# Loading v in longer runs, and transposing the exponentials through DRAM

## The chip, the cores and the metric

The kernel runs on one core of a Trainium2 chip. The metric is device time in microseconds (us), as a median of runs.

## The reference

Two attention steps and a feed-forward layer, in float32. For each of 8 batches and 8 heads, with 576 positions of 64 numbers, 32 learned rows p attend to k and v and give a packed result of 32 rows. Then each of the 576 rows of q attends to that packed result, which is both its keys and its values. The heads are laid side by side (512 numbers a position), and a layer follows with three input matrices of 512 x 768, of which the elementwise maximum is taken, and one output matrix.

```
p_packed = sm_attn(p, k, v)
out = sm_attn(q, p_packed, p_packed)
x = out.transpose(0, 2, 1, 3).reshape(B * S, H * D)
h = np.maximum(np.maximum(x @ w1, x @ w2), x @ w3)
return h @ w_out
```

## The kernel before

The work is cut by batch (8 of them). For each batch a chain of stages runs, each with a letter: S scores of p against k (line 253), A their softmax weights without the division (exponentials at line 271), then the exponentials are transposed, V their product with v (line 337), K the packed result turned, Q scores of q against it (line 366), B the second softmax (lines 389 to 412), P the packed result times the input weights (line 439), N the product of the second softmax with that (line 475, the largest part of TensorE's work), E the elementwise maximum, which moves N's sums out of PSUM into `r` (lines 486 and 489), H the operands of the output layer, O and F that layer and its stores (lines 544, 563, 573). N and O are done in two float32r parts each, a high and a low one.

The order of all instructions is written out by hand as two strings of words, START for batches 0 and 1 and the beginning of batch 2, and LOOP for each further pass. A word lets one stage take one step. A digit is the batch relative to the pass (X1 in LOOP is the spread of the next batch), and a letter v, g or a behind it chooses VectorE, GpSimd or ScalarE. Each engine works off its instructions in that order. Loads and stores stand in the same order and are all issued by SyncE.

The exponentials of batches 0 and 1 are transposed by TensorE (`turn`). Those of batches 2 to 7 go through `spread`, word X, in three steps. The first two let VectorE transpose all 32 x 32 blocks of one half of the heads (line 313) into the tile `x`. The third issues sixteen transfers (line 319) that move the blocks of `x`, partition group by partition group, into the tile `xt`, where they stand as V needs them. A block row there is 2 x 32 numbers, so each run of such a transfer is 256 B long. V multiplies slices of `xt` with v.

v of one batch and half of the heads is loaded by two transfers: `va`, 512 positions as 128 partitions of 4 KB, read as four runs of 1 KB a partition (line 165), and `vb`, the last 64 positions (line 166). The weights come as blocks of 512 KB, w00 to w52 for the input matrices and w60 to w65 for the output matrix (line 153), and are turned to float32 by four instructions each, on ScalarE (lines 188 and 193), VectorE (line 202) and GpSimd (line 206). q of one batch comes as two loads of 576 KB (line 174), called q20 and q21 for batch 2.

Tiles live in rotating buffers. k, v, q, `x`, `xt` and `r` share eight of them, and the staged weights share six with the output layer's operands. A load waits on SyncE until the earlier holder of its buffer has been read for the last time, and everything behind it on SyncE waits too. In START, around the third step of X2, SyncE's order is v21, v20, w42, w52, w51, the sixteen transfers, w64, w62, w65, q20, w63, w60, q21, w61.

Of the kernel before, what the change touches and what calls it, by code (L numbers as in the profile page):

```python
# [10 lines left out]
F32 = mybir.dt.float32  # L11
# [9 lines left out]
B, H, S, D, NP = 8, 8, 576, 64, 32  # L21
DM, DF = 512, 768
P = 128
G = 2
R = 2
# [3 lines left out]
SF = 4  # L29
# [3 lines left out]
NT = S // NP  # L33
# [3 lines left out]
NX, NB, NY = 6, 8, 21  # L37
# [51 lines left out]
def fused_kernel(ctx: ExitStack, tc: tile.TileContext, kp, qt, va, vb, wi, wo, out):  # L89
# [14 lines left out]
    nc = tc.nc  # L104

    const = ctx.enter_context(tc.tile_pool(name="const", bufs=1))
    pool = ctx.enter_context(tc.tile_pool(name="pool", bufs=1))
    ps_big = ctx.enter_context(tc.tile_pool(name="ps_big", bufs=2, space=PSUM))
    ps_moe = ctx.enter_context(tc.tile_pool(name="ps_moe", bufs=4, space=PSUM))

    ident = const.tile([P, P], F32, name="ident")
    make_identity(nc, ident)

# [48 lines left out]
    def load_v(b, g):  # L162
        u = b * G + g
        v = pool.tile([P, SF + 1, 256], F32, name=f"v{u}", tag="b", bufs=NB)
        nc.sync.dma_start(out=v[:, 0:SF, :], in_=va[u].rearrange("p (t x) -> p t x", x=256))
        nc.sync.dma_start(out=v[0:SR, SF, :], in_=vb[u])
        loaded["v", b, g] = v

# [72 lines left out]
    s1, a1, z1, a1t, av, pp, s2, a2 = {}, {}, {}, {}, {}, {}, {}, {}  # L241
# [63 lines left out]
    def spread(b):  # L305

        x = pool.tile([P, NT, R, NP], F32, name=f"x{b}", tag="b", bufs=NB)
        for r in range(R):
            nc.vector.transpose(out=x[:, :, r], in_=a1[b, r][0].rearrange("p (t y) -> p t y", y=NP))
            yield 1
        at = pool.tile([P, SF + 1, 4, R, NP], F32, name=f"xt{b}", tag="b", bufs=NB)
        for c in range(4):
            n = len(range(c, NT, 4))
            for i in range(4):
                nc.sync.dma_start(out=at[NP * c:NP * c + NP, 0:n, i], in_=x[NP * i:NP * i + NP, c::4])
        for r in range(R):  # L320
            a1t[b, r] = at[:, :, :, r]
        yield 0

    def values(b, rs):
# [280 lines left out]
    def weigh_and_turn(b, r):  # L605
# [4 lines left out]

    stages = {
        "S": scores, "A": weigh_and_turn, "Z": invert, "X": spread, "V": lambda b, *rs: values(b, rs), "K": packed, "Q": queries,
        "B": attend, "C": convert, "P": project, "N": layer_in, "E": maximum, "H": halves,
        "O": layer_out, "F": finish, "W": weights,
    }
    loads = {"k": load_k, "v": load_v, "q": load_q, "w": load_w}
    begun = {}

# [69 lines left out]
```

## Time and profile before

| | |
|---|---|
| median of 3 runs | 475.94 us (475.03 to 477.21) |
| span of the profiled execution | 471.1 us |
| TensorE matmul, weight load | 453.5 us (96%), 404.0 us (86%) |
| VectorE, ScalarE, GpSimd | 346.9 us (74%), 171.7 us (36%), 207.0 us (44%) |
| DMA | 55.66 MB, 36580 packets, of which 17328 under 512 B |

The profiled execution is one of its own. Its span, from its first to its last instruction, is what the profile's times refer to; its time beyond the span is not recorded, and the median lies 4.8 us above the span. In the rows, PE is TensorE's matmul, PEld its weight load, DVE VectorE, ACT ScalarE, POOL GpSimd, and SPq the queue of SyncE, which issues the DMAs. "a<-b" behind an instruction names the tile that it writes and those that it reads.

### The profile page before, as it was taken

The page shows a single profiled execution, that of the slowest core. Times are in us where ns is not written, and L with a number is a line of the kernel's source. Part 1 is how long each engine was busy: PE and PEld are TensorE (multiplying, and loading weights), DVE is VectorE, ACT ScalarE, POOL GpSimd, SP SyncE. Part 2 cuts the span into 40 slices and gives each one's busy share as a digit, 9 for nine tenths or more (in the row PEclk, how much of TensorE's full clock was granted, in tenths as well). Part 3 has the DMA queues.
Part 4 walks back from the last instruction along what each step waited for, and adds up shares of the span by engine and source line. Part 5 has one row for each costly group of instructions (what it writes and reads, how often), then busy time and mean ns, then how long its engine had stood idle before and what let it go on. Part 6 is the DMA issues. An engine that isn't in the chain of part 4 may idle for free.

```text
span 471.1 us, 11501 instructions
## 1 busy us (share of the span) xinstructions
PE 453.5 (96%) x4714; PEld 404.0 (86%) x4714; DVE 346.9 (74%) x727; ACT 171.7 (36%) x333; POOL 207.0 (44%) x180
## 2 busy tenths in 40 slices
PE   8669997999999999999999999999999999999996
PEld 4346985989899898989989898998989898998996
DVE  1698897899996668786777678776787668875652
ACT  3277866653441226122350225212260223402330
POOL 0346863767243055612563037421556036531542
PEclk9989999999999999999999999999999999999999
DMA  8998947003025540083303730064300820020002
GB/s 297 401 379 274 309 124 282 2 1 113 26 78 163 175 128 1 25 281 58 104 1 102 229 114 24 27 199 126 118 1 34 283 36 3 26 76 1 1 5 97
DMA packets 36580, 55.66 MB, mean 118 GB/s; under 512 B 17328, under 2 KB 27568, under 8 KB 36528
## 3 DMA queue, kind: packets, MB, share of 16 engines
q1 hardware_dynamic: 36528, 54.93, 35.8%
q8 instruction: 37, 0.61, 0.5%
q14 instruction: 15, 0.12, 0.1%
HBM read 41.94 MB, written 9.44 MB: 109 GB/s over the span
## 4 chain that ended last, share of the span: by engine, by line
PE 93%; DVE 3%; DMA 2%; ACT 1%; issue 0%; POOL 0%; POOLq 0%; DVEq 0%
PE mi L475 48%; PE mo L544 29%; PE pw L439 7%; PE s L253 2%; DMA q<-in_qt 2%; PE av L337 2%; PE s L366 2%; PE s L143 1%; PE tp L296 1%; DVE e L389 1%; PE tp L143 1%; DVE xt L218 0%; PE pa L143 0%; PE pa L337 0%; DVE w_sb L202 0%
## 5 line engine op out<-in xcount | busy, mean ns | idle before, releaser
L475 PE MATMUL mi<-a2h,ph 128*128 128x288 f32 x576 | 174.3, 303 | 2.6 <-DVE r L489 2.1
L475 PE MATMUL mi<-a2h,pl 128*128 128x288 f32 x576 | 170.1, 295 | 0.0
L475 PE MATMUL mi<-a2l,ph 128*128 128x288 f32 x576 | 170.1, 295 | 0.0
L475 PEld LDWEIGHTS mi<-a2h,ph 128*128 128x128 f32 x576 | 108.5, 188 | 18.2 <-issue 10.6
L475 PEld LDWEIGHTS mi<-a2h,pl 128*128 128x128 f32 x576 | 108.4, 188 | 0.0
L475 PEld LDWEIGHTS mi<-a2l,ph 128*128 128x128 f32 x576 | 108.4, 188 | 0.0
L489 DVE TENSOR_TENSOR r<-mi,r 128x288 f32<-128x288 f32 x192 | 83.2, 449 | 33.8 <-PE mi L475 31.0
L129 ACT COPY r<-mi 128x288 f32<-128x288 f32 x60 | 23.3, 399 | 121.4 <-PE mi L475 121.3
L452 DVE SCALAR_TENSOR_TENSOR pl<-pw,ph 128x768 fp32r<-128x768 f32 (+1 forms) x61 | 46.8, 775 | 4.4 <-ACT ph L450 3.7
L450 ACT ACTIVATE ph<-pw 128x768 fp32r<-128x768 f32 (+1 forms) x61 | 39.9, 675 | 19.6 <-PE pw L439 15.9
L544 PE MATMUL mo<-ych,xl 128*128 128x288 f32 x144 | 42.5, 295 | 0.0
L544 PE MATMUL mo<-ych,xh 128*128 128x288 f32 x144 | 42.4, 295 | 0.0
L544 PE MATMUL mo<-ycl,xh 128*128 128x288 f32 x144 | 42.4, 294 | 0.0
L134 POOL TENSOR_TENSOR yal<-r,yah 128x576 fp32r<-128x576 f32 x13 | 18.6, 1430 | 47.0 <-ACT yah L129 47.0
L439 PE MATMUL pw<-w_sb,pt 64*32 64x384 f32 x768 | 36.3, 487 | 1.0 <-POOL w_sb L206 1.0
L271 ACT ACTIVATE a<-s,nm 128x576 f32<-128x576 f32 x16 | 11.9, 743 | 66.8 <-DVE nm L267 66.8
L513 POOL TENSOR_TENSOR r<-r 128x288 f32<-128x288 f32 (+1 forms) x25 | 27.8, 1126 | 17.5 <-issue 9.0
L206 POOL TENSOR_TENSOR w_sb<-w_sb,wi 128x512 int32<-128x512 int32 x18 | 24.2, 1351 | 24.9 <-DVE z L282 11.8
L544 PE MATMUL mo<-yah,xh 128*128 128x288 f32 x96 | 28.8, 300 | 0.0
L131 POOL CAST yah<-r 128x576 fp32r<-128x576 f32 x6 | 4.0, 662 | 56.1 <-DVE r L513 56.1
L131 DVE COPY r<-mi 128x288 f32<-128x288 f32 x36 | 16.3, 454 | 16.5 <-PE mi L475 16.5
L544 PE MATMUL mo<-ybh,xl 128*128 128x288 f32 x96 | 28.3, 295 | 0.0
(121 smaller groups left out, 875.9 us busy)
## 6 DMA issues: line engine op xcount, KB each, us to landing
kt<-in_kp SPq DMA_DIRECT2D x16, 640.0 KB, 4.1
wi<-in_wi SPq DMA_DIRECT2D x18, 512.0 KB, 7.0
v<-in_va SPq DMA_DIRECT2D x16, 512.0 KB, 6.2
q<-in_qt SPq DMA_DIRECT2D x14, 576.0 KB, 7.6
wi<-in_wo SPq DMA_DIRECT2D x6, 512.0 KB, 5.0
out_t<-r SPq DMA_DIRECT2D x8, 288.0 KB, 2.3
out_t<-t SPq DMA_DIRECT2D x8, 288.0 KB, 2.3
out_t<-s SPq DMA_DIRECT2D x8, 288.0 KB, 2.7
```

What stands on the lines that cost most here:

```text
L129: e.copy(out=out, in_=src)
L131: e.tensor_copy(out=out, in_=src)
L134: on(default).tensor_tensor(out=lo, in0=src, in1=hi.bitcast(F32), op=ALU.subtract)
L206: nc.gpsimd.tensor_tensor(out=dst.bitcast(I32), in0=dst.bitcast(I32), in1=up, op=ALU.add)
L271: nc.scalar.activation(out=a.rearrange("p (a b) -> p a b", a=2), in_=s[:, :, 0:HS], func=AF.Exp, bias=nm, scale=SCALE, accum_out=z,)
L439: nc.tensor.matmul(out=ps[r][NP * n:NP * n + NP, 0:NW * P], lhsT=pt_sb[b % 2][o, NP * n:NP * n + NP], rhs=w_sb[o, j, n * NW * P:(n + 1) * ...
L450: nc.scalar.activation(out=hi[:, r], in_=x, func=AF.Copy, scale=2.0 ** -WS)
L452: nc.vector.scalar_tensor_tensor(out=lo[:, r], in0=x, scalar=2.0 ** -WS, in1=hi[:, r].bitcast(F32), op0=ALU.mult, op1=ALU.subtract,)
L475: nc.tensor.matmul(out=sums[b, j, hf, x][:, 0:HS], lhsT=w[:, r, x * P:(x + 1) * P], rhs=a[:, c], start=(r == 0 and n == 0), stop=(r == R - ...
L489: nc.vector.tensor_tensor(out=h, in0=sums[b, j, hf, i][:, 0:HS], in1=h, op=ALU.max)
L513: less = lambda out, x, y: on("g").tensor_tensor(out=out, in0=x, in1=y, op=ALU.subtract)
L544: nc.tensor.matmul(out=ps[:, 0:HS], lhsT=w[:, x, m * P:(m + 1) * P], rhs=h[:, z], start=(p == 0 and i == 0), stop=(p == NQ - 1 and i == 2),)
```

## The change

The load of `va` is written as one run of 4 KB a partition. In `spread`, each of the two transposes becomes four, one for every residue of the block number modulo 4, so that the blocks of one residue stand together in `x`. One transfer then stores `x` to a tile in DRAM, and four transfers, one for each residue, load from there into the four partition groups of `xt`, in runs of 1280 or 1024 B. The axes of `xt` are in another order, with the same 32 numbers in a row for V. The strings START and LOOP stay as they are.

```diff
+    dram = ctx.enter_context(tc.tile_pool(name="dram", bufs=1, space=bass.MemoryType.DRAM))
...
-        nc.sync.dma_start(out=v[:, 0:SF, :], in_=va[u].rearrange("p (t x) -> p t x", x=256))
+        nc.sync.dma_start(out=v[:, 0:SF, :].rearrange("p t x -> p (t x)"), in_=va[u])
...
         x = pool.tile([P, NT, R, NP], F32, name=f"x{b}", tag="b", bufs=NB)
+        first = [sum(len(range(k, NT, 4)) for k in range(c)) for c in range(5)]
         for r in range(R):
-            nc.vector.transpose(out=x[:, :, r], in_=a1[b, r][0].rearrange("p (t y) -> p t y", y=NP))
+            a = a1[b, r][0].rearrange("p (t y) -> p t y", y=NP)
+            for c in range(4):
+                nc.vector.transpose(out=x[:, first[c]:first[c + 1], r], in_=a[:, c::4])
             yield 1
-        at = pool.tile([P, SF + 1, 4, R, NP], F32, name=f"xt{b}", tag="b", bufs=NB)
+        kept = dram.tile([4, NP, NT, R, NP], F32, name=f"xk{b}")
+        nc.sync.dma_start(out=kept.rearrange("i p t r y -> (i p) (t r y)"), in_=x.rearrange("p t r y -> p (t r y)"))
+        at = pool.tile([P, 4, SF + 1, R, NP], F32, name=f"xt{b}", tag="b", bufs=NB)
         for c in range(4):
-            n = len(range(c, NT, 4))
-            for i in range(4):
-                nc.sync.dma_start(out=at[NP * c:NP * c + NP, 0:n, i], in_=x[NP * i:NP * i + NP, c::4])
+            n = first[c + 1] - first[c]
+            nc.sync.dma_start(
+                out=at[NP * c:NP * c + NP, :, 0:n].rearrange("p i t r y -> p i (t r y)"),
+                in_=kept[:, :, first[c]:first[c + 1]].rearrange("i p t r y -> p i (t r y)"),
+            )
         for r in range(R):
-            a1t[b, r] = at[:, :, :, r]
+            a1t[b, r] = at[:, :, :, r].rearrange("p i t y -> p t i y")
```

## Rows read from the trace of the kernel before

**Rows 1.** The page: busy us and shares; then TensorE's busy tenths in 40 slices.
```profile
PE 453.5 (96%) x4714; PEld 404.0 (86%) x4714; DVE 346.9 (74%) x727; ACT 171.7 (36%) x333; POOL 207.0 (44%) x180
PE   8669997999999999999999999999999999999996
```
**Rows 2.** Stretches: PE, PEld, DVE, ACT, POOL busy us (instructions), clock, DMA share, GB/s.
```profile
50.00:60.00 10.00, 10.00 (x97) 8.66 (x95) 8.17 (x19) 8.36 (x16) 8.07 (x7) 1.00 1.01 305
70.00:80.00 10.00, 7.31 (x143) 5.64 (x143) 7.18 (x16) 7.41 (x14) 4.25 (x4) 1.00 0.90 347
147.70:201.90 54.20, 54.20 (x590) 49.33 (x594) 40.22 (x85) 16.14 (x32) 22.69 (x20) 1.00 0.34 101
```
**Rows 3.** Waits of TensorE after 45 us: us in total, times, longest us.
```profile
PE mi L475 <- DVE r L489: 2.1, 2, 1.9
PE s L366 <- DMA q<-in_qt: 0.8, 1, 0.8
```
**Rows 4.** ScalarE in order of time: start, us, instruction [idle before it <- releaser].
```profile
70.39 0.71 ACT L188 ACTIVATE wi<-wi 128x512 f32<-128x512 f32 x1 [3.70 <-DMA wi<-in_wo]
...
77.18 0.68 ACT L188 ACTIVATE wi<-wi 128x512 f32<-128x512 f32 x1 [1.33 <-DMA wi<-in_wo]
```
**Rows 5.** VectorE and TensorE in order of time, around 75 us.
```profile
73.78 0.76 DVE L202 TENSOR_SCALAR xb<-wi 128x512 uint32<-128x512 uint32 x2 [2.82 <-ACT wi L188]
...
75.13 0.45 DVE L489 TENSOR_TENSOR r<-mi,r 128x288 f32<-128x288 f32 x1
...
75.63 0.40 PE L475 MATMUL mi<-a2h,ph 128*128 128x288 f32 x1 [1.91 <-DVE r L489]
...
79.80 1.17 PE L366 MATMUL s<-q,pt 64*32 64x288 f32 x24 [0.78 <-DMA q<-in_qt]
```
**Rows 6.** SyncE's issues in order of time, batch 2, then one of the loop.
```profile
49.44 3.21 SPq L153 DMA_DIRECT2D wi<-in_wi  x3
52.75 13.49 SPq L319 DMA_DIRECT2D xt<-x  x16
66.34 1.48 SPq L153 DMA_DIRECT2D wi<-in_wo  x3
68.01 0.33 SPq L174 DMA_DIRECT2D q<-in_qt  x1
68.39 1.12 SPq L153 DMA_DIRECT2D wi<-in_wo  x2
71.37 0.33 SPq L174 DMA_DIRECT2D q<-in_qt  x1
...
155.82 10.99 SPq L319 DMA_DIRECT2D xt<-x  x16
```
**Rows 7.** The chain that ended last, in order of time: start, us, what.
```profile
69.89 1.31 PE av L337 x73
...
71.37 8.38 DMA q<-in_qt
...
170.40 1.39 PE av L337 x80
```
**Rows 8.** DMA issues: count, KB each, median us from issue to landing.
```profile
v<-in_va SPq DMA_DIRECT2D x16, 512.0 KB, 6.2
...
wi<-in_wo SPq DMA_DIRECT2D x6, 512.0 KB, 5.0
out_t<-r SPq DMA_DIRECT2D x8, 288.0 KB, 2.3
```
**Rows 9.** VectorE's transposes by shape, with mean ns; four of them in order of time.
```profile
L389 DVE STREAM_TRANSPOSE e<-s 128x288 f32<-128x288 f32 x32 | 14.2, 467 | 2.6 <-PE s L366 2.6
L313 DVE STREAM_TRANSPOSE x<-a 128x576 f32<-128x576 f32 x12 | 9.3, 774 | 4.9 <-ACT a L271 4.9
...
40.48 1.56 DVE L389 STREAM_TRANSPOSE e<-s 128x288 f32<-128x288 f32 x4
```
**Rows 10.** Line 319 between 50 and 70 us: its transfers' time to landing.
```profile
DMA to landing us min/median/max: 1.9/2.1/7.5
```
**Rows 11.** GpSimd in order of time: the last step of one weight block.
```profile
66.67 1.70 POOL L206 TENSOR_TENSOR w_sb<-w_sb,wi 128x512 int32<-128x512 int32 x1 [1.09 <-ACT a2h L129]
```

## The prediction, made blind

> **What bounds the kernel now.** I read the busy shares first, then the stretches, then what TensorE waited for, then, backwards from each wait, the engines that caused it. TensorE is busy 96% of the span, and after the third of 40 slices only the seventh and the last are below 9 tenths [rows 1]. In the loop a pass of 54.20 us has TensorE busy for all of it, VectorE for 40.22 us and the DMA engines for a third; in 70 to 80 us TensorE is busy for only 7.31 of 10 us [rows 2]. So a change off TensorE can win nothing in the loop, and 2.69 us at 70 to 80 us. Those 2.69 us are two waits: 1.9 us for an eviction (`r`, line 489) and 0.8 us for the second load of q of batch 2 (q21) [rows 3].
>
> Both go back to late loads. ScalarE stood still 3.70 us until 70.39 us for the first block of the last weight matrix (w64), and again 1.33 us until 77.18 us for w63 [rows 4]. VectorE, in its program order, stood 2.82 us behind it and did the eviction that TensorE wanted only at 75.13 us [rows 5]. The loads were late because SyncE was issuing the sixteen transfers of the exponentials of batch 2 from 52.75 us for 13.49 us; w64, w62 and w65 followed at 66.34, q20 at 68.01, w63 and w60 at 68.39 us [rows 6]. From there the queue is full: q21, issued at 71.37 us when the attention of batch 2 had freed its buffer, took 8.38 us and landed at 79.75 us [rows 7].
>
> **The load of v.** 16 loads of 512 KB go from four runs of 1 KB a partition to one of 4 KB. The nearest row for one run of 4 KB and 512 KB is the weight load, 5.0 us to landing against 6.2 us for v [rows 8]: between 1.2 us gained and, since those loads met other traffic, as much lost a load. In the loop v is issued before 155.82 us and first used at 170.40 us [rows 6, 7]; that work of TensorE hides either. I take 0.
>
> **VectorE: eight transposes for two.** The columns stay the same (5, 5, 4 and 4 blocks of 32 for 18); six more instructions start per batch. A transpose of 576 columns takes 774 ns, one of 288 takes 467 ns, so 288 columns cost 307 ns and a start 160 ns when it stands alone; four in a row take 1.56 us, one each 0.36 us, which leaves 0.06 us a start [rows 9]. Six starts are 0.34 to 0.96 us a batch; a gain is excluded, since no column is saved. I take the lower value, since the four stand back to back. In the loop VectorE is idle 14 of 54.20 us [rows 2], and its evictions wait for TensorE, not the other way; the cost there is 0, and 0.2 us a pass if that cover were gone for one group. For batch 2 the two rounds lie at 45 and 50 us, where VectorE is nearly full: I charge 0.2 us (0 to 1.0).
>
> **DMAs: one store and four loads for sixteen.** SyncE issued a transfer in 13.49/16 = 0.84 us here and 10.99/16 = 0.69 us in the loop [rows 6]. Now it issues one store, waits for it, and issues four loads at about 0.65 us, a little under the loop's, which has some waiting in it: 2.6 us. The trace shows no store of 590 KB. Low bound: a store of 288 KB landed in 2.3 us in an empty queue [rows 8]. High bound: the first of the sixteen, behind three weight loads issued from 49.44 us, took 7.5 us [rows 10], and 550 KB more at the 0.305 MB/us of that stretch [rows 2] add 1.8 us: 9.3 us. The weight loads are still in front, so I take the high side less some of the time that the packets of 256 B cost: 8.8 us. The store then lands at 61.5, the loads are issued by 64.1, and w64 goes out then: 2.2 us earlier than at 66.34 us (1.7 us with the high bound, and 8.7 us with the low one: 52.75 + 2.3 + 2.6 = 57.65 us, where the staging buffers of w64 to w65 come free at about the same time).
>
> What waits behind SyncE's new wait: w64, w62, w65, q20, w63, w60, q21, in this order; all leave earlier in sum. q20 takes the buffer of the untransposed tile, which until now was read by sixteen transfers up to about 68 us and is now free when the store has landed. w60 needs the staging buffer of an earlier weight whose GpSimd step ends at 68.37 us (66.67 + 1.70) [rows 11], and q21 still needs the attention's end, 69.89 + 1.31 = 71.20 us [rows 7]; both stay where they are.
>
> What the 2.2 us buy: ScalarE's wait of 3.70 us shrinks to 1.5; VectorE's 2.82 to 0.6; the eviction is done at 75.58 - 2.2 = 73.4 us, before TensorE wants it at 75.63 - 1.91 = 73.7 us. The 1.9 us go. What is late next is q21: TensorE now reaches that wait at 79.80 - 0.78 - 1.91 = 77.1 us. Seven loads, 5 x 512 + 2 x 576 KB, ended at 79.75 us from a start at 66.34; started 2.2 us earlier, in a queue that never empties, they end at 77.5. Remaining wait 0.4 us of 0.78. So 1.9 + 0.4 - 0.2 = 2.1 us, and with the fewer packets of 256 B beside the weights I take 2.4 us. The four loads themselves: issued by 64.1, an estimated 2.8 us to landing (the 2.3 us of [rows 8] and something for four that share the queue), 66.9 us, where TensorE wants them at 69.89 us: 3 us of room. In the loop: store at 155.8, landed by 161.5 behind v and q, loads out by 164.1, landed by 167, wanted at 170.40 us: 3.4 us of room.
>
> The Trainium skill, DMA: Bandwidth & Descriptors, section on the anatomy of one DMA, says that most of the fixed cost of about 2 us is the receipt of the write, and that waiting for it "can cause a surprisingly long delay especially when the write target is HBM"; this change puts such a receipt in the path. The trace agrees on the size of the fixed part, with 2.3 us for a store to DRAM of 288 KB [rows 8]; no run here yet shows a load that waits for one. By the page's fit, as an estimate, the store would take 2.0 + 590/436 = 3.4 us in an empty queue, and the sum would come out some 0.3 us better than mine.
>
> **The sum.** Against the profiled execution, 471.1 us of span: 468.7 us. The median of the runs is 475.94 us, 4.8 us more, which lies around the span and stays: 473.5 us.
>
> **Rivals.** (a) Nothing gained: the store lands so late, beyond 63.5 us, or q21's transfer is so little helped that the wait only moves from the eviction to q21. For it: q21's own issue time doesn't move and it alone ended the stretch [rows 7]. Against it: six of the seven loads ahead of it leave earlier. The time: 475.9, up to 0.6 less. (b) Slower: the round trip through DRAM misses TensorE's turn. It decides at 3.4 us beyond my landing in the loop, 3.0 us in batch 2; from there every us is paid in each of six batches. With each of the two hops 2.3 us longer than I say, TensorE stands 1.2 us a batch: 6 x 1.2 = 7 us, and the gain at 70 to 80 us is kept only in part: 482 us. For it: the first of the sixteen waited 7.5 us behind other loads [rows 10], and the two hops add. Against it: sixteen issues took 10.99 us [rows 6] and the new chain has 5 us fewer of them. (c) All is gained and more: the store lands at the low bound, w64 leaves before 62 us, both waits go and the weights' chain after it has slack: 471.1 - 2.7 - 0.3 = 468.1, or 472.9 us, perhaps 472 with less crowding before 60 us.
>
> **How the numbers follow.** Forecast 0.50, (a) 0.25, (b) 0.08, (c) 0.17. What a measurement can tell from no change is about 0.5%, 2.4 us, so the forecast lies on that line. Its own range is 472.6 to 474.6. Half of the forecast's chance is faster by more than 0.5%, all of (c), and a little of (a): 0.46. (b) gives 0.07 slower, with 0.02 for an ordinary drift: 0.09. The rest, 0.45, is within. The range for 8 in 10 runs from (c)'s 472.0 to 476.6, the top of (a) with the spread of the runs before (475.03 to 477.21); (b) is left out.
>
> **What would show it.** Right: TensorE busy over 9.5 of 10 us at 70 to 80 us; the wait for `r` at line 489 gone; w64 out at about 64 us; loop passes still 54.2 us; 48 transposes of 260 to 330 ns. Wrong: waits of TensorE on the transposed tile at line 337 in the loop (b); q21 still landing near 79.7 us (a); VectorE late with evictions at 45 to 53 us, which would cost more than my 0.2 us.

## The result, and the profile after

| | before | after |
|---|---|---|
| median, beside each other on one chip (12 runs each) | 476.02 us (472.28 to 478.80) | 471.31 us (469.04 to 474.43) |
| ratio | | 0.991, 95% interval 0.989 to 0.994 |
| span of the profiled execution | 471.1 us | 472.7 us |

The change makes the kernel 4.1 us faster by the ratio (3.0 to 5.2 us by its interval). The time was forecast as 473.5 us with a range from 472.0 us: the direction was right, the gain too small, and the median lies 0.7 us under the range.

The two profiled spans say the opposite, so they have to be read with care. The page after, first busy us, then TensorE's busy tenths and granted clock in 40 slices:

```profile
PE 457.1 (97%) x4714; PEld 405.6 (86%) x4714; DVE 350.5 (74%) x763; ACT 171.8 (36%) x333; POOL 207.0 (44%) x180
...
PE   8769999999999999999999999999999999999996
...
PEclk9958999999999999999999999999999999999999
```

The seventh slice, 7 tenths before [rows 1], is full, but the third was granted only half the clock. The stretches after, with the columns of [rows 2]:

```profile
24.00:32.00 8.00, 5.12 (x58) 1.61 (x50) 5.90 (x20) 3.50 (x10) 2.58 (x3) 0.50 1.03 370
...
70.00:80.00 10.00, 10.00 (x157) 9.12 (x156) 9.29 (x21) 7.75 (x16) 6.21 (x6) 1.00 0.94 360
80.00:90.00 10.00, 9.80 (x113) 7.31 (x112) 9.32 (x18) 4.02 (x8) 5.92 (x6) 1.00 0.16 57
...
147.70:201.90 54.20, 54.20 (x584) 49.32 (x584) 39.33 (x91) 16.14 (x32) 23.50 (x21) 1.00 0.34 113
```

TensorE is busy for all of 70 to 80 us (7.31 us before), and a pass of the loop is as before. The stages lie later here, so that the wait for q21 falls into 80 to 90 us: 0.2 us of it are left on the matmul row. From 24 to 32 us the clock was 0.50, the lower of the two levels, 1.2 GHz. The same 32 score matmuls took 2.10 us there and 1.13 us in the loop; the chain after, in order of time:

```profile
27.71 2.10 PE s L255 x32
...
149.40 1.13 PE s L255 x32
```

SyncE's issues of batch 2 after, to be held against [rows 6]:

```profile
56.67 0.38 SPq L321 DMA_DIRECT2D xk<-x  x1
64.70 2.72 SPq L325 DMA_DIRECT2D xt<-xk  x4
67.52 1.33 SPq L155 DMA_DIRECT2D wi<-in_wo  x3
68.89 0.71 SPq L176 DMA_DIRECT2D q<-in_qt  x1
70.12 3.14 SPq L155 DMA_DIRECT2D wi<-in_wo  x2
75.87 0.33 SPq L176 DMA_DIRECT2D q<-in_qt  x1
```

The stages lie 3 to 5 us later than before: V of batch 1 began at 37.6 us, not 34.6, and V of batch 2 at 74.3, not 69.8. Counted from V of batch 2, w64 left 6.8 us ahead of it (67.52 us), where it had left 3.5 us ahead (66.34 us [rows 6]). To take the start out, the stretch from V of batch 2 (line 337 before) to S of batch 3 (line 253), called the middle below, is read in every kernel.

### The profile page after: what moved, and what is told of

It reads as the page before. It is cut to its first block, busy times and chain, and to the rows that moved or that the text cites. A ratio compares the mean times of both kernels' runs of the same rounds, so it can differ in the third digit from the quotient of the medians.

```text
span 472.7 us, 11472 instructions
## 1 busy us (share of the span) xinstructions
PE 457.1 (97%) x4714; PEld 405.6 (86%) x4714; DVE 350.5 (74%) x763; ACT 171.8 (36%) x333; POOL 207.0 (44%) x180
## 4 chain that ended last, share of the span: by engine, by line
PE 90%; DVE 4%; DMA 4%; ACT 1%; issue 1%; SPq 0%; DVEq 0%; ACTq 0%
PE mi L484 46%; PE mo L553 28%; PE pw L448 6%; PE s L255 2%; PE av L346 2%; PE s L375 2%; DMA wi<-in_wi 1%; DMA q<-in_qt 1%; DMA kt<-in_kp 1%; PE s L145 1%; DVE w_sb L204 1%; PE tp L145 1%; PE tp L298 1%; DVE e L398 1%; DVE xt L220 0%
## 5 line engine op out<-in xcount | busy, mean ns | idle before, releaser
L553 PE MATMUL mo<-yal,xh 128*128 128x288 f32 x96 | 28.3, 295 | 0.0
```

What stands on the lines that cost most here:

```text
L553: nc.tensor.matmul(out=ps[:, 0:HS], lhsT=w[:, x, m * P:(m + 1) * P], rhs=h[:, z], start=(p == 0 and i == 0), stop=(p == NQ - 1 and i == 2),)
```

## Experiments

Theory A: the gain is SyncE set free, so that the last weight loads and q leave earlier. B: a good part is the load of v. C: it is the packets of 256 B, not the issues. D: the spread between runs, and the profiles' disagreement, is the clock granted at the start. The middle is 77.8 us in the first profile of before (69.8 to 147.6) and 75.0 us after (74.3 to 149.3).

**The load of v alone.**

```diff
-        nc.sync.dma_start(out=v[:, 0:SF, :], in_=va[u].rearrange("p (t x) -> p t x", x=256))
+        nc.sync.dma_start(out=v[:, 0:SF, :].rearrange("p t x -> p (t x)"), in_=va[u])
```


> The kernel before with only the load of v changed (one run of 4 KB a partition). Theory A (the gain is SyncE set free around 55 to 66 us, so that the last weight loads and q20 leave earlier): ratio to before 0.998 to 1.002, and the two waits of TensorE at 70 to 80 us stay at 1.9 and 0.8 us. Theory B (half of the gain of 4.1 us is the load of v, which shortens the queue at the start): ratio 0.995 to 0.997, about 2 us.

Ratio to before 0.9986 (0.9963 to 1.0009), 474.87 us; the middle is 78.1 us, with waits of 1.9 and 0.9 us. No gain that can be measured: A stands. The interval still reaches into B's range, so B falls only with the next run.

**The exponentials alone.**

```diff
-        nc.sync.dma_start(out=v[:, 0:SF, :].rearrange("p t x -> p (t x)"), in_=va[u])
+        nc.sync.dma_start(out=v[:, 0:SF, :], in_=va[u].rearrange("p (t x) -> p t x", x=256))
```


> The changed kernel with the old load of v (four runs of 1 KB). Theory A: the whole gain, ratio 0.990 to 0.993, 3.3 to 4.5 us. Theory B: half of it, ratio 0.994 to 0.997.

Ratio 0.990 (0.986 to 0.994), 471.21 us, and a middle of 74.4 us. The whole gain, as A says; B's range lies outside the interval.

**Sixteen transfers with long runs.** The grouped transposes stay, the way through DRAM goes.

```diff
-    dram = ctx.enter_context(tc.tile_pool(name="dram", bufs=1, space=bass.MemoryType.DRAM))
...
-        kept = dram.tile([4, NP, NT, R, NP], F32, name=f"xk{b}")
-        nc.sync.dma_start(out=kept.rearrange("i p t r y -> (i p) (t r y)"), in_=x.rearrange("p t r y -> p (t r y)"))
...
         for c in range(4):
             n = first[c + 1] - first[c]
-            nc.sync.dma_start(
-                out=at[NP * c:NP * c + NP, :, 0:n].rearrange("p i t r y -> p i (t r y)"),
-                in_=kept[:, :, first[c]:first[c + 1]].rearrange("i p t r y -> p i (t r y)"),
-            )
+            for i in range(4):
+                nc.sync.dma_start(
+                    out=at[NP * c:NP * c + NP, i, 0:n].rearrange("p t r y -> p (t r y)"),
+                    in_=x[NP * i:NP * i + NP, first[c]:first[c + 1]].rearrange("p t r y -> p (t r y)"),
+                )
```


> The changed kernel without the way through DRAM: the grouped transposes, then sixteen transfers from x to xt in SBUF, but in runs of 1280 and 1024 B in place of 256 B. Theory A, by the number of issues (16 again, about 0.6 us each, q20 waits for the last): ratio 0.997 to 1.001 but for what v gives, and w64 leaves at 65 us or later. Theory C (the runs of 256 B fill the DMA engines and hold up the weights in front of them): ratio 0.991 to 0.995, with w42 to w51 landing about 1 us earlier.

Ratio 0.9998 (0.9968 to 1.0027), 475.14 us, and a middle of 77.8 us. Its SyncE, in order of time:

```profile
52.84 13.28 SPq L322 DMA_DIRECT2D xt<-x  x16
66.22 1.48 SPq L153 DMA_DIRECT2D wi<-in_wo  x3
```

The DMA engines had less to do (a share of 0.90 at 50 to 60 us against 1.01 [rows 2]), but sixteen issues hold SyncE for 13.28 us as they did for 13.49 us [rows 6]. The three weight loads in front landed between 0.2 us later and 0.4 us sooner after their issue, not the 1 us sooner that C asked for, and TensorE still waited 2.6 us for the eviction. C falls: it is the number of issues.

**The changed kernel, held up again.**

```diff
+        if b == 2:
+            spare = dram.tile([6, NP, NP], F32, name="spare")
+            for i in range(6):
+                nc.sync.dma_start(out=spare[i], in_=x[0:NP, i, 0])
         for r in range(R):
             a1t[b, r] = at[:, :, :, r].rearrange("p i t y -> p t i y")
```


> The changed kernel with six small stores (32 partitions of 128 B, from x to a spare DRAM tile) issued behind the four loads, in batch 2 alone: SyncE is held for 2.5 to 3.5 us and x is read until then, as by the sixteen transfers. Nothing else is changed. Theory A: 1.5 to 2.7 us of the gain go, ratio 0.995 to 0.998, and the waits of TensorE for the eviction or for q21 come back at 70 to 80 us. Theories B and C: ratio unchanged at 0.990 to 0.993.

Ratio 0.9968 (0.9942 to 0.9994), 474.73 us beside the 471.21 us of the exponentials alone on the same chip: six small stores in one batch give back 3.5 us, more than the 1.5 to 2.7 us expected. Its SyncE, and its waits of TensorE after 70 us (us in total, times, longest):

```profile
64.52 2.59 SPq L325 DMA_DIRECT2D xt<-xk  x4
67.15 2.75 SPq L332 DMA_DIRECT2D spare<-x  x6
70.43 1.31 SPq L155 DMA_DIRECT2D wi<-in_wo  x3
71.92 0.33 SPq L176 DMA_DIRECT2D q<-in_qt  x1
```
```profile
PE mi L488 <- DVE r L502: 2.4, 2, 2.1
```

The eviction's wait is back with 2.1 us, the middle is 77.3 us, and nothing but SyncE's time, the buffer of `x` and 24 KB of traffic was touched. That settles A. Between time and buffer it is SyncE's own time: w64, w62 and w65 stand in front of q20 and don't need the buffer of `x`, and q20 went out 0.2 us behind them here (71.74 to 71.92 us), as it did before (67.82 to 68.01 us [rows 6]).

**Fillers at the start, in both kernels.** Three words R6 in START, each six blocks of 128 columns into a free PSUM tile that nobody reads, in idle gaps of TensorE at 18 to 31 us.

```diff
-V01 Z01 V01 K0 w01 K0v C01 I2 Q0 B010 B010 q011 Q0 C01 k11 k10 C01 B001 B001 B000 B011 B000 B011 w02 B000v
-B011v C00 k21 B010 C01 B010 B010 B000 B000 B000v I5 S1 B011 k20 w12 C02 C02 I3 S2 B001 A10 B001 C02 C02 P00
+V01 Z01 V01 K0 w01 K0v C01 I2 Q0 B010 B010 q011 Q0 R6 C01 k11 k10 C01 B001 B001 B000 B011 B000 B011 w02 B000v
+B011v C00 k21 B010 C01 B010 B010 B000 B000 B000v I5 S1 R6 B011 k20 w12 C02 C02 I3 S2 B001 A10 B001 C02 C02 P00 R6
...
+            if kind == "R":
+                kept_idle, idle[0] = idle[0], int(name[1:])
+                rouse(ps_moe.tile([P, 512], F32, name=f"fill{len(filled)}", tag="moe"))
+                filled.append(0)
+                idle[0] = kept_idle
+                continue
```


> The kernel before with six more blocks of filler matmuls (128 columns each, into a free PSUM tile that nobody reads) in each of three idle gaps of TensorE at 18 to 31 us. Theory D (the spread of the runs, and the 3 us by which the profiled execution of before lies under the median, are the clock granted to TensorE at 16 to 40 us): granted clock 1.00 from 16 to 40 us, median 1 to 3 us lower, ratio 0.994 to 0.998, spread under 3 us in place of 7. If D is wrong: ratio 0.999 to 1.003, since the fillers lie in gaps, and the same spread.

> The changed kernel with the same fillers. Theory A with D: 3.0 to 3.6 us below the run of before with fillers, which is the cost of the two waits at 70 to 80 us counted by what the weight loads waited (2.1 and 1.3 us); ratio to before 0.986 to 0.991. If the change also shortens the start by itself, the difference between the two filled kernels is 4 us or more.

Before with fillers: 472.38 us (6 runs, 471.39 to 473.37), ratio 0.992 (0.989 to 0.994). After with fillers: 468.61 us (4 runs, 468.38 to 468.91), ratio 0.984 (0.9815 to 0.9859). The kernel before ran beside them at 476.06 us (475.07 to 477.59). The fillers alone give 3.7 us, more than the 1 to 3 us expected, so the median bears D out; for the spread it is open, since the runs beside these spread over 2.5 us only, not 7. Both ratios lie below the expected ranges. The two filled kernels differ by 3.77 us, above the 3.0 to 3.6 us of A and under the 4 us that would have meant a shorter start. Their stretches, the kernel before with fillers first:

```profile
16.00:24.00 8.00, 6.71 (x77) 3.19 (x78) 6.49 (x17) 2.85 (x7) 2.65 (x3) 1.00 1.02 410
24.00:32.00 8.00, 6.20 (x64) 2.79 (x63) 7.38 (x27) 5.84 (x15) 3.98 (x5) 1.00 1.03 365
...
70.00:80.00 10.00, 7.29 (x115) 5.24 (x103) 6.73 (x16) 7.19 (x14) 3.64 (x4) 1.00 0.83 320
```
```profile
70.00:80.00 10.00, 10.00 (x153) 7.93 (x149) 9.32 (x23) 5.73 (x12) 5.21 (x5) 1.00 0.49 172
```

The granted clock is 1.00 in these stretches, and V of batch 2 begins at 69.15 and 69.12 us. From there it is the change alone: the middle takes 77.9 and 74.15 us, 3.75 us apart, which is the whole 3.77 us between the medians. TensorE's matmuls, from V of batch 2 to the first product after the second half of Q's scores, show where; the kernel before with fillers, then the changed one with fillers:

```profile
69.15 1.38 PE L337 MATMUL av<-v,xt 128*32 128x64 f32 x73
...
75.04 0.40 PE L475 MATMUL mi<-a2h,ph 128*128 128x288 f32 x1 [1.92 <-DVE r L489]
...
77.74 0.69 PE L366 MATMUL s<-q,pt 64*32 64x288 f32 x8
79.22 1.18 PE L366 MATMUL s<-q,pt 64*32 64x288 f32 x24 [0.79 <-DMA q<-in_qt]
80.33 0.40 PE L475 MATMUL mi<-a2h,ph 128*128 128x288 f32 x1
```
```profile
69.12 1.38 PE L346 MATMUL av<-v,xt 128*32 128x64 f32 x73
...
75.42 1.20 PE L375 MATMUL s<-q,pt 64*32 64x288 f32 x32
76.55 0.40 PE L484 MATMUL mi<-a2h,ph 128*128 128x288 f32 x1
```

From V to the scores it is 8.59 against 6.30 us: the eviction's wait costs 2.29 us. From the scores to the next product it is 2.59 against 1.13 us: the wait for q21 costs 1.46 us. Together that is 3.75 us, the whole difference, while the idle times in the matmul row add up to 2.71 us (1.92 and 0.79). What the weight loads of TensorE waited for in the first of them, at 69 to 85 us:

```profile
PEld mi L475 <- DVE r L489: 2.2, 1, 2.2
PEld mi L475 <- issue: 1.7, 3, 0.6
PEld s L366 <- DMA q<-in_qt: 1.3, 1, 1.3
```

In the changed kernel with fillers both named waits are gone, 2.2 + 1.3 = 3.5 us of the 3.75; "issue" falls by 0.5 us to 1.2, and 0.5 us of a wait for VectorE are new. SyncE of the one, and of the other, says where they went:

```profile
52.02 13.24 SPq L319 DMA_DIRECT2D xt<-x  x16
65.36 1.49 SPq L153 DMA_DIRECT2D wi<-in_wo  x3
```
```profile
52.21 0.39 SPq L321 DMA_DIRECT2D xk<-x  x1
59.29 1.75 SPq L325 DMA_DIRECT2D xt<-xk  x4
61.15 1.33 SPq L155 DMA_DIRECT2D wi<-in_wo  x3
62.51 0.71 SPq L176 DMA_DIRECT2D q<-in_qt  x1
63.75 4.27 SPq L155 DMA_DIRECT2D wi<-in_wo  x2
70.66 0.33 SPq L176 DMA_DIRECT2D q<-in_qt  x1
```

The loads went out 7.1 us after the store, took SyncE 1.75 us, and w64 left 4.2 us earlier. The changed kernel with fillers is the version that beats both.

**Both kernels once more.** No edit.

> The kernel before once more, for a second profile. Theory D: span 473 to 475 us where the first profile had 471.1, and the whole difference lies before the first values product of batch 1 (34.6 us in the first profile), with a granted clock under 0.9 at 16 to 32 us; from the product of batch 2 to the scores of batch 3 again 77.8 us. Otherwise the difference lies in the later stretches.

> The changed kernel once more, for a second profile. Theory A: from the product of batch 2 to the scores of batch 3 74.4 to 75.0 us, whatever the clock at the start; the start takes 36 to 40 us by the clock granted there.

Before again: span 475.7 us. Of the 4.6 us that it is longer than the first profile, 2.1 us lie before V of batch 2 (1.3 us before V of batch 1), so the start explains only a part, and D is wrong for the rest: the middle took 80.3 us, where 77.8 was expected. Its stretches and its weight loads' waits at 69 to 85 us:

```profile
32.00:40.00 8.00, 8.00 (x114) 7.45 (x113) 5.39 (x13) 5.64 (x14) 3.33 (x4) 0.68 0.79 314
...
70.00:80.00 10.00, 6.98 (x127) 5.64 (x126) 5.86 (x14) 5.39 (x10) 3.59 (x4) 0.91 0.97 362
80.00:90.00 10.00, 10.00 (x102) 7.60 (x102) 7.91 (x17) 4.34 (x8) 5.01 (x6) 0.75 0.23 73
```
```profile
PEld mi L475 <- DVE r L489: 2.1, 1, 2.1
PEld mi L475 <- ACT r L129: 1.4, 1, 1.4
```

Here the late weights cost two waits for evictions, and the clock fell to 0.91 and 0.75 in the stretches that hold these waits and follow them. Of the 2.5 us that the middle is longer, 2.2 us are in TensorE's busy time (77.06 against 74.87 us), at the lower clock. After again: span 470.7 us, V of batch 1 at 38.0 us, the middle 74.15 us with the clock at 1.00.

## Why the prediction fell short

- **Which waits, and why: right.** Two waits at 70 to 80 us, from the last weights and q, behind SyncE. Held up again, the eviction's wait came back. Set free, both were gone in three of four profiles; in the first one after, 0.7 us of the weight loads' wait for q21 stayed, and the middle was 0.9 us longer than with both gone (75.0 against 74.15 us).
- **The failing step: the price of the two waits.** The prediction took 2.69 us, TensorE's idle time on the matmul row at 70 to 80 us, for all that could be won, 1.9 and 0.8 us [rows 2, 3]. Measured from the start of one stage to the start of the next, the same two waits cost 2.29 and 1.46 us. The first eight score matmuls show how: they are drawn as busy for 0.69 us, while 32 in a row take 1.20 us, so a part of the wait for q21 stands as busy time. The Trainium skill, Perfetto Trace Analysis (Identifying the Most-Contended Engine), says that matmul busy time is a bad measure of how close TensorE is to its limit, and that the busy share of the weight loads (LDWEIGHTS) is one to use instead. This trace agrees that the matmul row misleads: it has 2.7 us of these waits, the weight-load row 3.5 us, and the cost was 3.75 us.
- **"What the 2.2 us buy": mis-sized too.** The store to DRAM was put at 8.8 us and took 6.9 to 8.1 us in batch 2; the four loads were put at 2.6 us and held SyncE for 1.75 us with fillers, 2.6 to 2.7 us without. w64 left 4.2 us earlier with fillers, not 2.2. So the wait for q21, of which 0.4 us were to stay, went too. In the terms of the sum: 2.3 us in place of 1.9, 1.5 in place of 0.4, and nothing is left for the 0.2 us charged to VectorE or the 0.3 us for fewer small packets.
- **The anchor: wrong by 3 us.** I put 4.8 us around the span. The changed kernel's runs have 1.7 to 1.8 us there (474.43 against 472.7; 469.04 against 467.2). So, by the same 1.8 us, the profiled execution of before took about 472.9 us, 3 us under the median. That shifts no difference by itself, but the execution was a fast one: in the second profile, with 475.7 us of span, the middle is 2.5 us longer.
- **What is left over.** I forecast 2.4 us; the filled pair shows 3.77 us, and the ratio without fillers, 4.1 us with an interval from 3.0 to 5.2, agrees with that. Whether the clock that falls after the waits adds to it there, as the second profile of before suggests, rests on one profile and stays open. The mean clock listed with each run hints at it: at 0.993, the three runs of before had 473.92 to 474.79 us and the four of the exponentials alone 470.19 to 471.39 us on the same chip, 3.1 us apart at the median, where all runs of the two are 4.4 us apart. Open too is the start: in the three profiles with both changes and without fillers, V of batch 1 began at 37.6 to 38.1 us, in the five others without fillers at 34.5 to 35.9 us, and with fillers at 33.83 and 33.85 us. Why is not shown.
- **Load of v: right**, no change. **VectorE: right about a start.** Four transposes took 0.95 us where one took 0.77, and the low bound of 0.06 us a start holds: 3 x 0.06 = 0.18. With fillers V of batch 2 begins at the same time in both kernels, so nothing of the 0.2 us shows. No pass of the loop is longer.
- **Rival (b), slower: no.** The store took 4.0 us or more in every kept trace, and 4.5 us in the pass that stores at 157.68 us; the last of its loads landed at 167.5 us, and V came at 172.0 us. So the low end, 2.3 us, was never reached. The estimate of 3.4 us for an empty queue, from the fit in the Trainium skill, DMA: Bandwidth & Descriptors (Anatomy of one DMA), was not tested by any run. That section is about transfers that GpSimd issues, while SyncE issues these, and the 2.3 us that the prediction set beside its fixed part [rows 8] are the whole time of a store of 288 KB.
- **(c)** came nearest to what happened: both waits went, though the store did not land at its low bound.

## What to carry to other kernels

When a kernel is bound by one engine, look for the few microseconds where it isn't, and follow them back to the issuing queue: here a burst of sixteen small transfers delayed loads behind it by about 4 us, and longer packets in the same sixteen transfers changed nothing. Price a wait of TensorE from the start of the stage before it to the start of the stage behind it, or by its weight loads, not by the idle time of the matmul row alone. Before a profiled span is set against a median, see what clock that execution was granted and take a second profile.

## What the runs showed of the hardware

SyncE needed about 0.6 us for each transfer from SBUF to SBUF (601 ns at the median) and 0.33 to 0.43 us for most that load the same data from DRAM (423 ns at the median). In one pass of the loop a store of 576 KB and the loads that read it back took 9.8 us together (157.68 to 167.5 us), less than the 10.99 us in which the sixteen transfers were only issued [rows 6]. A matmul can be drawn as busy while the next one waits: eight score matmuls 0.69 us in front of a wait, 32 of them 1.20 us in a row. Eighteen blocks of filler matmuls took 3.7 us off the kernel before (476.06 to 472.38 us): TensorE had work in its gaps, and the granted clock stayed at 1.00 from 16 to 40 us.
